# Request a weight load early, spread the Fourier chunks anew, and compute a tile plan with slots on partitions

## The chip, the cores and the metric

The kernel runs on one core of a Trainium2 chip. Its engines are TensorE (PE, matrix products), VectorE (DVE), ScalarE (ACT), GpSimd (POOL) and SyncE (SP, which issues most of the DMAs). Each engine has its own instruction queue and works through it in order; an instruction starts when the semaphores it waits for are set. The metric is device time in microseconds, the median of several runs.

## The reference

The input x is 8 x 3072 x 256. The reference takes the real part of a two-dimensional Fourier transform over each batch, 24,576 rows of 256 in all. Then come two layers. The first is a switched mixture of experts with a skip:

```python
do_compute = x @ w_skip > 0
e_idx = argmax(x[do_compute] @ w_gate)          # 8 experts, one is chosen
h = maximum(xc[mask] @ w1[e], 0)                # 256 -> 1024
y[mask] = gate_w * (h @ w2[e]);  out[do_compute] = xc + y
```

The second is applied to every row: h = x @ w_in (256 -> 2048), g = P(h) / Q(h) with a cubic P and Q = 1 + |b0||h| + |b1|h^2, and g @ w_out (2048 -> 256).

## The kernel before, in words

All products are made from f16 pairs (high and low part), three products for one.

**Fourier stage (lines 455 to 692).** A loop over n runs 12 steps for each of the 8 batches, plus two. In step gp of batch bb, `s2` transforms the features of a pair of column groups (product into u, ACT evicts o2h, DVE makes o2l), `s3` finishes the sequence direction two steps later, and its rows are written to a row buffer, one of ten places, of which seven lie in the memory mw that later holds expert weights. `s1` makes a chunk of the first stage for the next batch, eight chunks to a batch; `go` (line 635) says in which steps. ACT writes the chunk's high half (`s1_hi`, line 242) and, in the step after the chunk, the low half o1l (`s1_lo`, line 253). The tile u has three buffers, used by `s1` and `s2` in turn. `decode_steps` (line 391) converts w_in and w_out and the first two experts into f16 pairs in DRAM (WD), 65 small steps spread over 84 loop steps; each piece is loaded on SP into one of two buffers wr.

**Routing.** When a batch is done, `route_steps` (line 334) runs one segment per loop step beside the next batch: expert choice on DVE, a counting product on PE (line 354), the row numbers si, and then 24 scatters of rows to XS in DRAM by POOL (line 380), two in a step, three for the last batch. A `tick` (line 379) is a copy on POOL that reads an earlier step's o2h and so holds the scatters back. The last batch's segments run in the second part.

**Second part (from line 696).** The loop over i (line 1196) makes the second layer in steps of 256 of the 2048 columns: `z_mm1` (u), T, Y, V on ACT and DVE, gh and gl on DVE, a subtraction V on POOL, and `z_mm2` five steps later into accz, with the result ob evicted at the end of a tile. Between these it runs `all_moe`, the experts on halves of 256 rows: a DMA of rows xm, weights into mw (`load_moe`, line 880), a split and a DMA transpose (`moe_begin`), products e and acc. `last` is the routing of the last batch, `planning` the generator `make_plan` (line 727). The plan says for each of 52 slots which rows and which expert come next, and later the same for up to 116 left-over slots; it is computed on DVE, on one partition, with the slots along the free dimension (1x416 and 1x928 elements). Between both plans `fill` (line 902) copies rows on SP when all scatters are issued. The first three halves of expert 0 are loaded before the plan is known; the first load of weights, `WD[0]` (line 889), goes into the place of four of the row buffers.

The order on each engine is the order of these calls; no planner changes it.

Of the kernel before, what the change touches and what calls it, by code (L numbers as in the profile page):

```python
# [33 lines left out]
S1 = 52  # L34
# [18 lines left out]
def constants():  # L53
# [57 lines left out]
    c["lt8"] = (np.arange(8)[None, :] < np.arange(8)[:, None]).astype(np.float32).reshape(1, 64)  # L111
# [20 lines left out]
def program(tc, x, w_skip, w_gate, w1, w2, w_in, w_out, a, b, f1, cs, tw, tok, ut, small, lt8, slot, out):  # L132
# [3 lines left out]
    with es:  # L136
# [197 lines left out]
        def route_steps(bb, new_u, per=2):  # L334
# [16 lines left out]
            yield  # L351
            u = new_u()
# [18 lines left out]
            yield  # L371
# [3 lines left out]
            yield  # L375
            for g in range(NG):
                if g % per == 0 and bb < B - 1:

                    pool.tensor_copy(out=tick[:].bitcast(F16)[:, 0:1], in_=seen[0][:, 0, 0:1])
                i = pool.indirect_dma_start(out=XS[:, :], out_offset=IndirectOffsetOnAxis(ap=si[:, g:g + 1], axis=0),  # L380
                                            in_=rws[g // 4][:, g % 4, :], in_offset=None, bounds_check=NROWS - 1, oob_is_err=False)
                if scat:
                    tc.declare_no_dep(i.ins, group="scat", reason="every slot is given once")
                tc.add_to_no_dep_group("scat", i.ins)
                if bb >= 4:
                    tc.add_to_no_dep_group("scat7", i.ins)
                scat.append(i.ins)
                if g % per == per - 1:
                    yield

        def decode_steps():
# [10 lines left out]

            nxt = load(0)
# [29 lines left out]
            def load_e(n):  # L433
                e, k = divmod(n, 4)
                t = wp.tile([128, 2048], I32, tag="wr", bufs=2, name="wr")[:].bitcast(F32)[:, 0:1024]
                if k < 2:
                    sp.dma_start(out=t, in_=w1[e, k * 128:k * 128 + 128, :])
                else:
                    sp.dma_start(out=t.rearrange("p (c n) -> p c n", c=4), in_=w2[e, (k - 2) * 512:(k - 1) * 512, :].rearrange("(c p) n -> p c n", p=128))
                return t  # L440

            nxt = load_e(0)
# [268 lines left out]
        pll = pool_of("pll", 1)  # L711
# [14 lines left out]

        def make_plan():
            def v(n, name):
                return pl.tile([1, n], F32, name=name)

            pf = v(NC_, "pf")
            sl_t, lt_t = v(NL + S1, "sl_t"), v(64, "lt_t")
            lim, fs = sl_t[:, NL:NL + S1], v(1, "fs")
            sp.dma_start(out=sl_t[:], in_=slot)
            sp.dma_start(out=lt_t[:], in_=lt8)
            cnt, nt, pad, cx, px, ce, r2 = (v(n, nm) for n, nm in ((9, "cnt"), (8, "nt"), (8, "pad"), (8, "cx"), (8, "px"), (8, "ce"), (8, "r2")))
            ti = pl.tile([1, 8], I32, name="ti")
            m8, mt, pt, tk, tf, of, st, t1 = (v(n, nm) for n, nm in ((64, "m8"), (1, "mt"), (1, "pt"), (1, "tk"), (1, "tf"), (1, "of"), (1, "st"), (1, "t1")))
            ind = rt[0:1, 0:NL * 8]
            sA, sB, sC = v(NL, "sA"), v(NL, "sB"), v(NL, "sC")  # L740
            sm = pll.tile([1, NL], F32, name="sm")
# [3 lines left out]
            def floor_of(dst, src, add, shift):  # L745
                n = src.shape[-1]
                ts(out=ti[:, 0:n], in0=src, scalar1=float(add), scalar2=None, op0=ALU.add)
                ts(out=ti[:, 0:n], in0=ti[:, 0:n], scalar1=shift, scalar2=None, op0=ALU.logical_shift_right)
                dve.tensor_copy(out=dst, in_=ti[:, 0:n])

            def before(dst, src):
                m = m8[:].rearrange("o (e f) -> o e f", f=8)
                tt(out=m, in0=src[:, None, :].to_broadcast([1, 8, 8]), in1=lt_t[:].rearrange("o (e f) -> o e f", f=8), op=ALU.mult)
                dve.tensor_reduce(out=dst[:, :, None], in_=m, op=ALU.add, axis=AX.X)

            tt(out=cnt[:], in0=carry[0:1, :], in1=smt[0:1, 0:9], op=ALU.subtract)
            tt(out=cnt[:], in0=cnt[:], in1=smt[0:1, 9:18], op=ALU.mult)
# [16 lines left out]
            stt(out=r2[:], in0=cx[:], scalar=-float(HALF), in1=smt[0:1, 9:17], op0=ALU.mult, op1=ALU.mult)  # L774
            tt(out=r2[:], in0=r2[:], in1=smt[0:1, 26:34], op=ALU.add)

            def skip_row(dst, s, limit, unit, tmp):
                ts(out=tmp, in0=s, scalar1=limit, scalar2=None, op0=ALU.is_lt)
                ts(out=dst, in0=s, scalar1=float(unit), scalar2=nsk, op0=ALU.mult, op1=ALU.subtract)
                tt(out=dst, in0=dst, in1=tmp, op=ALU.mult)  # L780
                ts(out=dst, in0=dst, scalar1=nsk, scalar2=float(SKIP0), op0=ALU.add, op1=ALU.add)

            def halves(rows, experts, s, n, at):

                b3 = [1, n, 8]
                i3 = ind[:, 0:8 * n].rearrange("o (m e) -> o m e", e=8)
                v3 = rt[0:1, at:at + 8 * n].rearrange("o (m e) -> o m e", e=8)
                s3 = s[:, :, None].to_broadcast(b3)
                tt(out=i3, in0=s3, in1=cx[:, None, :].to_broadcast(b3), op=ALU.is_ge)
                tt(out=v3, in0=s3, in1=ce[:, None, :].to_broadcast(b3), op=ALU.is_ge)  # L790
                yield
                tt(out=i3, in0=i3, in1=v3, op=ALU.subtract)
                stt(out=v3, in0=s3, scalar=float(HALF), in1=smt[0:1, None, 9:17].to_broadcast(b3), op0=ALU.mult, op1=ALU.mult)
                tt(out=v3, in0=v3, in1=r2[:, None, :].to_broadcast(b3), op=ALU.add)
                yield
                tt(out=v3, in0=v3, in1=i3, op=ALU.mult)
                dve.tensor_reduce(out=sA[:, 0:n, None], in_=v3, op=ALU.add, axis=AX.X)
                yield
                tt(out=v3, in0=i3, in1=smt[0:1, None, 34:42].to_broadcast(b3), op=ALU.mult)
                dve.tensor_reduce(out=experts[:, :, None], in_=v3, op=ALU.add, axis=AX.X)  # L800
                yield
                ts(out=sC[:, 0:n], in0=s, scalar1=mt[:], scalar2=of[:], op0=ALU.subtract, op1=ALU.add)
                skip_row(rt[0:1, at:at + n], sC[:, 0:n], tk[:], HALF, sB[:, 0:n])
# [10 lines left out]
            stt(out=m8[:, 0:8], in0=pad[:], scalar=-float(HALF), in1=smt[0:1, 50:58], op0=ALU.add, op1=ALU.mult)  # L814
            tt(out=px[:], in0=px[:], in1=m8[:, 0:8], op=ALU.add)
            stt(out=px[:], in0=tk[:].to_broadcast([1, 8]), scalar=float(HALF), in1=px[:], op0=ALU.mult, op1=ALU.add)
            ts(out=pf[:, C_SRC:C_SRC + 8], in0=px[:], scalar1=nsk, scalar2=float(SKIP0), op0=ALU.min, op1=ALU.add)
            tt(out=pad[:], in0=cnt[:, 0:8], in1=smt[0:1, 9:17], op=ALU.mult)
            tt(out=pf[:, C_DST:C_DST + 8], in0=pad[:], in1=smt[0:1, 42:50], op=ALU.add)
            ts(out=pf[:, C_DUM:C_DUM + 1], in0=nsk, scalar1=float(SKIP0), scalar2=None, op0=ALU.add)  # L820
            out_now(C_SRC, C_DUM + 1)
            yield
            skip_row(pf[:, C_SKIP:C_SKIP + S2], sl_t[:, 0:S2], tf[:], TILE, sB[:, 0:S2])
            out_now(C_SKIP, C_SRC)
            yield from halves(pf[:, C_ROW:C_ROW + S1], pf[:, C_EXP:C_EXP + S1], sl_t[:, 0:S1], S1, 576)

            ex = pf[:, C_EXP:C_EXP + S1]
            tt(out=sA[:, 0:S1], in0=ex, in1=lim, op=ALU.is_le)
            dve.tensor_reduce(out=fs[:], in_=sA[:, 0:S1], op=ALU.min, axis=AX.X)
# [9 lines left out]
            tt(out=fs[:], in0=fs[:], in1=co[0:1, 16:17], op=ALU.mult)  # L839
            fast = fs[:]  # L840
            tt(out=of[:], in0=of[:], in1=fast, op=ALU.mult)
            ts(out=st[:], in0=fast, scalar1=float(S1), scalar2=None, op0=ALU.mult)
            ts(out=sm[:], in0=sl_t[:, 0:NL], scalar1=st[:], scalar2=None, op0=ALU.add)
            yield from halves(pf[:, C_LROW:C_LROW + NL], pf[:, C_LEXP:C_LEXP + NL], sm[:], NL, NL * 8)
# [4 lines left out]
            floor_of(pf[:, C_REM:C_REM + 1], t1[:], 1, 1)  # L849
# [30 lines left out]
        def load_moe(m):  # L880
# [418 lines left out]
```

## Time and profile before

| | us |
|---|---|
| median of 3 runs (3045.4 to 3047.98) | 3046.88 |
| profiled execution | 3047.06 |
| its span, first to last instruction | 3045.3 |
| PE busy (96% of the span) | 2911.8 |
| DVE busy (92%) | 2797.9 |
| ACT busy (84%) | 2549.3 |
| POOL busy (45%) | 1384.9 |

Busy shares are averages over stages with different limits: each stage is read from its own rows. The span and the profiled execution differ by what lies before the first and after the last instruction, 1.8 us.

### The profile page before, as it was taken

How to read it: one execution, taken by the hardware profiler on the slowest of the kernel's cores; microseconds unless marked ns; L12 is line 12 of the kernel's file. 1: busy time of each engine (PE TensorE's matmuls, PEld its weight loads, DVE VectorE, ACT ScalarE, POOL GpSimd, SP SyncE). 2: the span in 40 equal slices, each digit the busy share in tenths (PEclk: the TensorE clock that was granted, in tenths of full speed). 3: DMA queues.
4: the chain of work that ended last, by engine and by line, in shares of the span. 5: the costliest groups of instructions: out<-in, count | busy, mean ns of one | idle time of the engine just before them, and what ended most of it. 6: DMA issues, size and time to landing. Idle time of an engine off the chain costs nothing.

```text
span 3045.3 us, 57147 instructions
## 1 busy us (share of the span) xinstructions
PE 2911.8 (96%) x22994; PEld 2132.2 (70%) x22994; DVE 2797.9 (92%) x2909; ACT 2549.3 (84%) x2835; POOL 1384.9 (45%) x861
## 2 busy tenths in 40 slices
PE   7898868999899999999999999999999999999995
PEld 6777746776677777777777777777777777777764
DVE  6888769999999999999999999998999989999896
ACT  6887767888788988988889888888888888888884
POOL 0476665444344444444444444434444444444444
PEclk9999989999999999999999999999999999999998
DMA  7666653223121331323222121121122111210100
GB/s 207 192 183 187 240 150 88 77 63 111 43 70 46 94 91 42 71 72 102 56 56 84 53 46 36 50 76 33 38 63 71 28 44 27 91 39 25 36 15 15
DMA packets 230370, 236.87 MB, mean 78 GB/s; under 512 B 166995, under 2 KB 190932, under 8 KB 227156
## 3 DMA queue, kind: packets, MB, share of 16 engines
q1 hardware_dynamic: 209364, 174.23, 21.3%
q0 software_dynamic: 18432, 50.55, 4.7%
q10 hardware_dynamic: 2304, 8.39, 0.7%
q8 instruction: 181, 2.97, 0.4%
q14 instruction: 89, 0.73, 0.1%
HBM read 190.69 MB, written 77.05 MB: 88 GB/s over the span
## 4 chain that ended last, share of the span: by engine, by line
PE 75%; DVE 13%; ACT 4%; DMA 4%; issue 3%; POOL 1%; SPq 0%; ACTq 0%; POOLq 0%; DVEq 0%
PE accz L948 28%; PE u L938 27%; PE acc L948 8%; PE e L938 8%; DVE gh L1042 3%; PE u L269 2%; DVE T L1024 2%; DVE V L1047 2%; DMA out<-ob,ids 2%; DVE gl L1054 1%; PE v L319 1%; DVE wo L211 1%; DVE o2l L274 1%; ACT wo L204 1%; ACT o2h L273 0%
## 5 line engine op out<-in xcount | busy, mean ns | idle before, releaser
L1048 POOL TENSOR_TENSOR V<-T,V 128x1024 f32<-128x1024 f32 x384 | 913.7, 2379 | 1374.0 <-DVE V L1047 1373.6
L938 PE MATMUL u<-turned,wi 128*128 128x512 f16 x4608 | 1064.3, 381 | 20.6 <-DVE T L1024 17.8
L948 PE MATMUL accz<-wo,gh 128*128 128x256 f16 x6144 | 1034.9, 274 | 9.2 <-ACT ob L1070 9.2
L948 PE MATMUL accz<-wo,gl 128*128 128x256 f16 x3072 | 841.1, 274 | 20.0 <-DVE gl L1054 17.7
L1042 DVE SCALAR_TENSOR_TENSOR gh<-T,co,Y 128x1024 f16<-128x1024 f32 x384 | 803.2, 2092 | 0.0
L938 PEld LDWEIGHTS <-wi 128*128 128x128 f16 x4608 | 452.6, 98 | 490.0 <-issue 31.8
L1022 ACT ACTIVATE T<-u,co 128x1024 f32<-128x1024 f32 x384 | 462.9, 1205 | 328.8 <-PE u L938 210.5
L948 PEld LDWEIGHTS <-gh 128*128 128x128 f16 x6144 | 603.7, 98 | 162.6 <-issue 10.3
L1024 DVE SCALAR_TENSOR_TENSOR T<-T,co,u 128x1024 f32<-128x1024 f32 x384 | 487.6, 1270 | 66.0 <-ACT Y L1023 65.5
L1054 DVE SCALAR_TENSOR_TENSOR gl<-V,co,Y 128x1024 f16<-128x1024 f32 x384 | 489.1, 1274 | 28.8 <-POOL V L1048 28.8
L1047 DVE SCALAR_TENSOR_TENSOR V<-V,co,gh 128x1024 f32<-128x1024 f32 x384 | 490.3, 1277 | 0.0
L1028 ACT ACTIVATE V<-Y,co 128x1024 f32<-128x1024 f32 x384 | 440.4, 1147 | 23.7 <-DVE gl L1054 23.7
L1032 ACT ACTIVATE Y<-V,co 128x1024 f32<-128x1024 f32 x384 | 441.2, 1149 | 0.0
L1023 ACT ACTIVATE Y<-u,co 128x1024 f32<-128x1024 f32 x384 | 426.3, 1110 | 0.0
L1036 ACT ACTIVATE Y<-Y 128x1024 f32<-128x1024 f32 x384 | 404.3, 1053 | 0.0
L948 PEld LDWEIGHTS <-gl 128*128 128x128 f16 x3072 | 301.7, 98 | 59.9 <-DVE gl L1054 21.6
L938 PE MATMUL e<-turned,mw 128*128 128x256 f16 x2496 | 307.7, 273 | 15.0 <-DMA turned<-rows 15.0
L948 PE MATMUL acc<-mw,hh 128*128 128x256 f16 x1664 | 278.1, 273 | 0.0
L938 PEld LDWEIGHTS <-mw 128*128 128x128 f16 x2496 | 244.7, 98 | 44.2 <-DMA mw<-wd 12.2
L1071 POOL DMA_INDIRECT out<-ob,ids x192 | 232.8, 1213 | 64.2 <-issue 44.7
L948 PE MATMUL acc<-mw,hl 128*128 128x256 f16 x832 | 226.8, 273 | 0.0
L948 PEld LDWEIGHTS <-hh 128*128 128x128 f16 x1664 | 162.8, 98 | 18.9
(207 smaller groups left out, 2739.1 us busy)
## 6 DMA issues: line engine op xcount, KB each, us to landing
mw<-wd SPq DMA_DIRECT2D x50, 2048.0 KB
wi<-in_x SPq DMA_DIRECT2D x64, 384.0 KB
xm<-xs SPq DMA_DIRECT2D x52, 258.0 KB
wf<-in_moe_w SPq DMA_DIRECT2D x48, 256.0 KB
wd<-ws SPq DMA_DIRECT2D x48, 256.0 KB
xt<-xs SPq DMA_DIRECT2D x22, 516.0 KB
wd<-ws ACTq DMA_DIRECT2D x16, 512.0 KB
wr<-in_moe_w_in SPq DMA_DIRECT2D x4, 1024.0 KB
```

What stands on the lines that cost most here:

```text
L938: pe.matmul(u[:, s, :], lhsT=sta, rhs=mv[:, :, k, :], start=(n == 0), stop=(n == 5))
L948: pe.matmul(acc[:, r, :], lhsT=sta[:, c], rhs=mv, start=(first and r % 2 == 0 and s == 0 and n == 0), stop=(last and s == nf - 1 and n == ...
L1022: act.activation(d["T"], d["u"], AF.Square, scale=A[0], bias=A[1])
L1023: act.activation(d["Y"], d["u"], AF.Abs, scale=A[4])
L1024: dve.scalar_tensor_tensor(out=d["T"], in0=d["T"], scalar=A[2], in1=d["u"], op0=ALU.add, op1=ALU.mult)
L1028: act.activation(d["V"], d["Y"], AF.Square, bias=A[5])
L1032: act.activation(d["Y"], d["V"], AF.Ln, bias=A[6])
L1036: act.activation(d["Y"], d["Y"], AF.Exp, scale=-1.0)
L1042: dve.scalar_tensor_tensor(out=h[:], in0=d["T"], scalar=A[a0], in1=d["Y"], op0=ALU.add, op1=ALU.mult)
L1047: dve.scalar_tensor_tensor(out=d["V"], in0=d["V"], scalar=A[c], in1=h[:], op0=ALU.add, op1=ALU.mult)
L1048: pool.tensor_tensor(out=d["V"], in0=d["T"], in1=d["V"], op=ALU.subtract)
L1054: dve.scalar_tensor_tensor(out=l[:], in0=d["V"], scalar=A[a0], in1=d["Y"], op0=ALU.add, op1=ALU.mult)
```

## The change

Four edits. (1) The routing gets one more step between the one-hot and the counting product, except for batch 6 (`hurry`), which loses three steps, has no ticks and issues four scatters in a step. (2) The decoder's first load is issued in step 0, and the first load of the expert weights in its last decode piece. (3) Chunks are made in steps 0-2, 4-6, 8 and 9 of a batch instead of 0, 1, 3, 4, 6, 7, 9 and 10. (4) In the second part the constants sl_t and lt_t are loaded at the head, the first expert's weights in two DMAs, and the plan is computed with one slot to a partition; its two columns (row, expert) go to DRAM and come back as rows. One scalar takes the same way before the second plan. Constants for it: `small[:, 58]` is the partition's number, and lt8 is repeated on 128 partitions.

```diff
@@ route_steps
+            hurry = bb == B - 2
...
-            yield
+            if not hurry:
+                yield
...
             yield
+            if not hurry:
+                yield
             u = new_u()
...
+            if hurry:
+                per = 4
             for g in range(NG):
-                if g % per == 0 and bb < B - 1:
+                if g % per == 0 and bb < B - 2:
@@ decode_steps
             nxt = load(0)
-            pend = None
+            yield
             for n in range(8):
                 t = nxt
-                if n + 1 < 8:
-                    nxt = load(n + 1)
+                nxt = load(n + 1) if n + 1 < 8 else load_e(0)
...
-            nxt = load_e(0)
             for n in range(4 * EARLY):
@@ Fourier loop
-            go = c1 < 8 * B and gp % 3 != 2
+            go = c1 < 8 * B and gp % 4 != 3 and gp < 10
...
+            if n == 0:
+                next(prep)
@@ second part
+        sl_t = pl.tile([1, NL + S1], F32, name="sl_t")
+        lt_t = pl.tile([128, 64], F32, name="lt_t")
+        sp.dma_start(out=sl_t[:], in_=slot)
+        sp.dma_start(out=lt_t[:], in_=lt8)
+        PD = tc.dram_tile([128, 2], F32, name="pd")
+        PF = tc.dram_tile([1, 1], F32, name="pfs")
@@ make_plan (its tiles are now [128, n])
+            def halves(s, n, to):
+                sH, sC, hA, hB, ro = (hw[:, k:k + 1] for k in range(5))
+                ts(out=hi[:], in0=cx[:], scalar1=s, scalar2=None, op0=ALU.is_le)
+                stt(out=hi[:], in0=ce[:], scalar=s, in1=hi[:], op0=ALU.is_gt, op1=ALU.mult)
+                ts(out=sH, in0=s, scalar1=float(HALF), scalar2=None, op0=ALU.mult)
+                stt(out=hv[:, 0:8], in0=smt[:, 9:17], scalar=sH, in1=r2[:], op0=ALU.mult, op1=ALU.add)
+                yield
+                dve.tensor_copy(out=hv[:, 8:16], in_=smt[:, 34:42])
+                v3 = hv[:].rearrange("p (t e) -> p t e", e=8)
+                tt(out=v3, in0=v3, in1=hi[:, None, :].to_broadcast([128, 2, 8]), op=ALU.mult)
+                dve.tensor_reduce(out=hc[:, :, None], in_=v3, op=ALU.add, axis=AX.X)
+                ts(out=sC, in0=s, scalar1=mt[:], scalar2=of[:], op0=ALU.subtract, op1=ALU.add)
+                yield
+                skip_row(ro, sC, tk[:], HALF, hA)
+                stt(out=hB, in0=s, scalar=mt[:], in1=ro, op0=ALU.is_ge, op1=ALU.mult)
+                tt(out=hc[:, 0:1], in0=hc[:, 0:1], in1=hB, op=ALU.add)
+                sp.dma_start(out=PD[:, :], in_=hc[:])
+                sp.dma_start(out=to.rearrange("o (c n) -> o c n", c=2), in_=PD[0:n, None, :].rearrange("n o c -> o c n"))
...
+            yield from halves(smt[:, 58:59], S1, pf[0:1, C_ROW:C_ROW + 2 * S1])
+            for _ in range(3):
+                yield
...
+            sp.dma_start(out=PF[:, :], in_=fs[0:1])
+            sp.dma_start(out=fs[:], in_=PF[0:1, 0:1].to_broadcast([128, 1]))
+            for _ in range(3):
+                yield
...
+            yield from halves(st[:], NL, pf[0:1, C_LROW:C_LROW + 2 * NL])
+            for _ in range(3):
+                yield
@@ load_moe
-                    sp.dma_start(out=w, in_=WD[0])
+                    for k in (0, 2):
+                        sp.dma_start(out=w[:, k:k + 2], in_=WD[0, :, k:k + 2])
```

## Rows read from the trace of the kernel before

**Rows 1.** Windows by stage: bounds, length, busy us (instructions) by engine, clock, DMA.
```profile
0.00:394.80 394.80, 343.10 (x4153) 284.97 (x4154) 302.59 (x717) 303.94 (x506) 194.86 (x236) 0.97 0.65 198
394.80:511.40 116.60, 81.79 (x506) 50.74 (x505) 90.76 (x153) 73.16 (x78) 65.70 (x59) 0.87 0.39 119
...
730.00:810.00 80.00, 67.39 (x489) 47.29 (x487) 79.35 (x83) 58.01 (x60) 29.11 (x16) 1.00 0.24 74
810.00:2950.00 2140.00, 2138.30 (x15834) 1548.97 (x15832) 2046.16 (x1733) 1869.74 (x1940) 953.97 (x481) 1.00 0.20 56
```

**Rows 2.** Windows of steps 5 to 8 of batches 0, 1, 2, 5.
```profile
49.49:70.90 21.41, 16.56 (x178) 13.15 (x176) 11.52 (x19) 14.12 (x23) 0.00 (x0) 0.84 0.77 246
102.47:115.93 13.46, 12.95 (x158) 10.70 (x156) 12.97 (x41) 11.80 (x20) 4.52 (x6) 1.00 0.51 146
146.33:162.15 15.82, 13.32 (x158) 10.90 (x158) 14.21 (x42) 12.87 (x22) 9.39 (x12) 1.00 0.54 163
...
282.03:304.01 21.98, 15.28 (x177) 12.20 (x175) 12.72 (x42) 13.92 (x22) 8.56 (x13) 0.84 0.63 196
```

**Rows 3.** Waits, 30 to 345 us: who for whom, total us, times, longest.
```profile
DVE wf L415 <- DMA wr<-in_moe_w_in: 6.5, 1, 6.5
...
ACT ws L448 <- DMA wr<-in_moe_w: 5.7, 1, 5.7
```

**Rows 4.** Timeline of PE: start, length, instruction, idle time before and its releaser.
```profile
212.53 0.40 PE L269 MATMUL u<-f2t,o1h 128*128 128x276 f16 x2 [0.60 <-ACT o1l L253]
...
216.95 0.29 PE L269 MATMUL u<-f2t,o1l 128*128 128x276 f16 x1 [1.23 <-ACT o1l L253]
...
431.56 2.72 PE L938 MATMUL e<-turned,mw 128*128 128x256 f16 x12 [15.01 <-DMA turned<-rows]
```

**Rows 5.** Waits of PE, 30 to 396 us.
```profile
PE u L269 <- ACT o1l L253: 11.6, 13, 1.2
```

**Rows 6.** Waits of PE, 395 to 520 us.
```profile
PE u L938 <- DVE T L1024: 9.3, 5, 3.0
PE accz L948 <- ACT ob L1070: 5.2, 1, 5.2
...
PE acc L354 <- DVE rt L350: 2.4, 1, 2.4
```

**Rows 7.** Timeline of POOL, scatters from 371 to 416 us.
```profile
371.40 1.13 POOL L380 DMA_INDIRECT xs<-mw,rt  x1 [6.87 <-DMA xt<-xs]
...
415.84 0.97 POOL L380 DMA_INDIRECT xs<-mw,rt  x1 [0.30 <-issue]
```

**Rows 8.** Timeline of SP's issues, 418 to 505 us.
```profile
418.74 0.33 SPq L889 DMA_DIRECT2D mw<-wd  x1
...
421.83 4.44 SPq L929 DMA_TRANSPOSE turned<-rows  x1
...
426.85 0.23 SPq L735 DMA_DIRECT2D lt_t<-const_lt  x1
...
489.64 0.64 SPq L906 DMA_DIRECT2D xs<-dum  x1
...
503.98 0.38 SPq L885 DMA_DIRECT2D xm<-xs  x1
```

**Rows 9.** Timeline of DVE at the first plan.
```profile
431.76 0.21 DVE L753 TENSOR_TENSOR m<-nt,lt_t 1x64 f32<-1x64 f32 x1 [7.46 <-DMA lt_t<-const_lt]
```

**Rows 10.** DVE by line, 731 to 783 us: busy us, mean ns, idle before.
```profile
L1042 DVE SCALAR_TENSOR_TENSOR gh<-T,co,Y 128x1024 f16<-128x1024 f32 x5 | 6.3, 1267 | 0.0
...
L790 DVE TENSOR_TENSOR rt<-sm,ce 1x928 f32<-1x928 f32 x1 | 3.3, 3278 | 0.0
...
L789 DVE TENSOR_TENSOR rt<-sm,cx 1x928 f32<-1x928 f32 x1 | 1.1, 1111 | 0.0
...
L846 DVE TENSOR_TENSOR t<-t,of 1x1 f32<-1x1 f32 x1 | 0.1, 148 | 0.0
```

**Rows 11.** DVE by line, 520 to 1000 us.
```profile
L1042 DVE SCALAR_TENSOR_TENSOR gh<-T,co,Y 128x1024 f16<-128x1024 f32 x70 | 147.2, 2103 | 0.0
```

More of the change, by code (lines that the diff above doesn't have):

```diff
@@ L110, in constants @@
     c["small"] = np.broadcast_to(small, (128, 64)).copy()
-    c["lt8"] = (np.arange(8)[None, :] < np.arange(8)[:, None]).astype(np.float32).reshape(1, 64)
+    c["small"][:, 58] = np.arange(128)
+    c["lt8"] = np.broadcast_to((np.arange(8)[None, :] < np.arange(8)[:, None]).astype(np.float32).reshape(1, 64), (128, 64)).copy()
     c["slot"] = np.concatenate([np.arange(NL), [limit(m) for m in range(S1)]]).astype(np.float32).reshape(1, NL + S1)
@@ L370, in route_steps @@
                 dve.tensor_scalar(out=carry[:, 0:1], in0=carry[:, 0:1], scalar1=float(R1 * HALF), scalar2=None, op0=ALU.max)
-            yield
+            if not hurry:
+                yield
             dve.tensor_tensor(out=rk, in0=rk, in1=oh, op=ALU.mult)
@@ L401, in load, with load_e @@
                 return t
+            def load_e(n):
+                e, k = divmod(n, 4)
+                t = wp.tile([128, 2048], I32, tag="wr", bufs=2, name="wr")[:].bitcast(F32)[:, 0:1024]
+                if k < 2:
+                    sp.dma_start(out=t, in_=w1[e, k * 128:k * 128 + 128, :])
+                else:
+                    sp.dma_start(out=t.rearrange("p (c n) -> p c n", c=4), in_=w2[e, (k - 2) * 512:(k - 1) * 512, :].rearrange("(c p) n -> p c n", p=128))
+                return t
             nxt = load(0)
-            pend = None
+            yield
             for n in range(8):
                 t = nxt
-                if n + 1 < 8:
-                    nxt = load(n + 1)
+                nxt = load(n + 1) if n + 1 < 8 else load_e(0)
                 v = t[:].rearrange("p (n two) -> p n two", two=2)
@@ L710, in program @@
         pl = pool_of("pl", 1)
-        pll = pool_of("pll", 1)
         obp = pool_of("obp", 1)
@@ L725, in program @@
         plan = pl.tile([1, NC_], I32, name="plan")
+        sl_t = pl.tile([1, NL + S1], F32, name="sl_t")
[4 more added lines that the diff above has]
+        PF = tc.dram_tile([1, 1], F32, name="pfs")
         def make_plan():
             def v(n, name):
-                return pl.tile([1, n], F32, name=name)
-            pf = v(NC_, "pf")
-            sl_t, lt_t = v(NL + S1, "sl_t"), v(64, "lt_t")
+                return pl.tile([128, n], F32, name=name)
+            pf = pl.tile([1, NC_], F32, name="pf")
+            hi, hv, hc, hw = v(8, "hi"), v(16, "hv"), v(2, "hc"), v(5, "hw")
             lim, fs = sl_t[:, NL:NL + S1], v(1, "fs")
-            sp.dma_start(out=sl_t[:], in_=slot)
-            sp.dma_start(out=lt_t[:], in_=lt8)
             cnt, nt, pad, cx, px, ce, r2 = (v(n, nm) for n, nm in ((9, "cnt"), (8, "nt"), (8, "pad"), (8, "cx"), (8, "px"), (8, "ce"), (8, "r2")))
-            ti = pl.tile([1, 8], I32, name="ti")
+            ti = pl.tile([128, 8], I32, name="ti")
             m8, mt, pt, tk, tf, of, st, t1 = (v(n, nm) for n, nm in ((64, "m8"), (1, "mt"), (1, "pt"), (1, "tk"), (1, "tf"), (1, "of"), (1, "st"), (1, "t1")))
-            ind = rt[0:1, 0:NL * 8]
-            sA, sB, sC = v(NL, "sA"), v(NL, "sB"), v(NL, "sC")
-            sm = pll.tile([1, NL], F32, name="sm")
+            sA, sB = v(S1, "sA"), v(S1, "sB")
             nsk = cnt[:, 8:9]
@@ L746, in floor_of @@
                 n = src.shape[-1]
-                ts(out=ti[:, 0:n], in0=src, scalar1=float(add), scalar2=None, op0=ALU.add)
-                ts(out=ti[:, 0:n], in0=ti[:, 0:n], scalar1=shift, scalar2=None, op0=ALU.logical_shift_right)
-                dve.tensor_copy(out=dst, in_=ti[:, 0:n])
+                t = ti[0:src.shape[0], 0:n]
+                ts(out=t, in0=src, scalar1=float(add), scalar2=None, op0=ALU.add)
+                ts(out=t, in0=t, scalar1=shift, scalar2=None, op0=ALU.logical_shift_right)
+                dve.tensor_copy(out=dst, in_=t)
             def before(dst, src):
                 m = m8[:].rearrange("o (e f) -> o e f", f=8)
-                tt(out=m, in0=src[:, None, :].to_broadcast([1, 8, 8]), in1=lt_t[:].rearrange("o (e f) -> o e f", f=8), op=ALU.mult)
+                tt(out=m, in0=src[:, None, :].to_broadcast([128, 8, 8]), in1=lt_t[:].rearrange("o (e f) -> o e f", f=8), op=ALU.mult)
                 dve.tensor_reduce(out=dst[:, :, None], in_=m, op=ALU.add, axis=AX.X)
-            tt(out=cnt[:], in0=carry[0:1, :], in1=smt[0:1, 0:9], op=ALU.subtract)
-            tt(out=cnt[:], in0=cnt[:], in1=smt[0:1, 9:18], op=ALU.mult)
+            tt(out=cnt[:], in0=carry[:], in1=smt[:, 0:9], op=ALU.subtract)
+            tt(out=cnt[:], in0=cnt[:], in1=smt[:, 9:18], op=ALU.mult)
             floor_of(nt[:], cnt[:, 0:8], HALF - 1, 8)
@@ L773, in make_plan @@
             yield
[L774 to L775 removed]
+            stt(out=r2[:], in0=cx[:], scalar=-float(HALF), in1=smt[:, 9:17], op0=ALU.mult, op1=ALU.mult)
+            tt(out=r2[:], in0=r2[:], in1=smt[:, 26:34], op=ALU.add)
             def skip_row(dst, s, limit, unit, tmp):
+                n = nsk[0:s.shape[0]]
                 ts(out=tmp, in0=s, scalar1=limit, scalar2=None, op0=ALU.is_lt)
[L779 removed]
+                ts(out=dst, in0=s, scalar1=float(unit), scalar2=n, op0=ALU.mult, op1=ALU.subtract)
@@ L813, in make_plan @@
             yield
[L814 to L820, printed above, removed]
+            one = nsk[0:1]
+            stt(out=m8[0:1, 0:8], in0=pad[0:1], scalar=-float(HALF), in1=smt[0:1, 50:58], op0=ALU.add, op1=ALU.mult)
+            tt(out=px[0:1], in0=px[0:1], in1=m8[0:1, 0:8], op=ALU.add)
+            stt(out=px[0:1], in0=tk[0:1].to_broadcast([1, 8]), scalar=float(HALF), in1=px[0:1], op0=ALU.mult, op1=ALU.add)
+            ts(out=pf[:, C_SRC:C_SRC + 8], in0=px[0:1], scalar1=one, scalar2=float(SKIP0), op0=ALU.min, op1=ALU.add)
+            tt(out=pad[0:1], in0=cnt[0:1, 0:8], in1=smt[0:1, 9:17], op=ALU.mult)
+            tt(out=pf[:, C_DST:C_DST + 8], in0=pad[0:1], in1=smt[0:1, 42:50], op=ALU.add)
+            ts(out=pf[:, C_DUM:C_DUM + 1], in0=one, scalar1=float(SKIP0), scalar2=None, op0=ALU.add)
             out_now(C_SRC, C_DUM + 1)
             yield
-            skip_row(pf[:, C_SKIP:C_SKIP + S2], sl_t[:, 0:S2], tf[:], TILE, sB[:, 0:S2])
+            skip_row(pf[:, C_SKIP:C_SKIP + S2], sl_t[:, 0:S2], tf[0:1], TILE, sB[0:1, 0:S2])
             out_now(C_SKIP, C_SRC)
-            yield from halves(pf[:, C_ROW:C_ROW + S1], pf[:, C_EXP:C_EXP + S1], sl_t[:, 0:S1], S1, 576)
+            yield from halves(smt[:, 58:59], S1, pf[0:1, C_ROW:C_ROW + 2 * S1])
+            for _ in range(3):
+                yield
             ex = pf[:, C_EXP:C_EXP + S1]
-            tt(out=sA[:, 0:S1], in0=ex, in1=lim, op=ALU.is_le)
-            dve.tensor_reduce(out=fs[:], in_=sA[:, 0:S1], op=ALU.min, axis=AX.X)
+            tt(out=sA[0:1], in0=ex, in1=lim, op=ALU.is_le)
+            dve.tensor_reduce(out=fs[0:1], in_=sA[0:1], op=ALU.min, axis=AX.X)
             tt(out=ex, in0=ex, in1=lim, op=ALU.min)
@@ L837, in make_plan @@
                 yield
-            tt(out=fs[:], in0=fs[:], in1=co[0:1, 16:17], op=ALU.mult)
+            sp.dma_start(out=PF[:, :], in_=fs[0:1])
+            sp.dma_start(out=fs[:], in_=PF[0:1, 0:1].to_broadcast([128, 1]))
+            for _ in range(3):
+                yield
+            tt(out=fs[:], in0=fs[:], in1=co[:, 16:17], op=ALU.mult)
             fast = fs[:]
             tt(out=of[:], in0=of[:], in1=fast, op=ALU.mult)
-            ts(out=st[:], in0=fast, scalar1=float(S1), scalar2=None, op0=ALU.mult)
-            ts(out=sm[:], in0=sl_t[:, 0:NL], scalar1=st[:], scalar2=None, op0=ALU.add)
-            yield from halves(pf[:, C_LROW:C_LROW + NL], pf[:, C_LEXP:C_LEXP + NL], sm[:], NL, NL * 8)
+            stt(out=st[:], in0=fast, scalar=float(S1), in1=smt[:, 58:59], op0=ALU.mult, op1=ALU.add)
+            yield
+            yield from halves(st[:], NL, pf[0:1, C_LROW:C_LROW + 2 * NL])
+            for _ in range(3):
+                yield
             tt(out=t1[:], in0=mt[:], in1=tk[:], op=ALU.add)
```

34 lines of the change are left out of this document (2 added, 32 removed).

## The prediction

> **What bounds the kernel now.** I read the windows by stage first. From 810 to 2950 us TensorE is busy 2138.3 of 2140, so time can only be won where PE stands idle or runs at its lower clock. Three stretches do that [rows 1]: the Fourier stage (PE 343.1 busy of 394.8 us), the opening of the second part (81.79 of 116.6, mean granted clock 0.87) and the second plan (67.39 of 80). The change edits these three. In each I then read who ends PE's waits. The profiled execution took 3047.06 us (span 3045.3), the median of the runs is 3046.88; the sum starts from 3047.
>
> **Weight loads in the Fourier stage.** Two loads are requested in the step that uses them: the first of w_in, for which DVE stands 6.5 us, and the first of w1, for which ACT stands 5.7 us [rows 3]. Both engines are in order, so o2h and o2l behind them, and then PE, stand too. Steps 5 to 8 of those two batches took 21.41 and 21.98 us; the same steps of the four batches between took 13.46 to 15.82, mean 14.84 [rows 2]. The excess is 6.6 + 7.1 = 13.7 us, and the granted clock is 0.84 there against 1.00. After the change the first load leaves SP in step 0, five steps earlier, the other six decode yields earlier, and neither takes a buffer that is still being read. On SP it passes a few x loads, which are requested four chunks ahead. I take the waits themselves, 6.5 + 5.7 = **12.2 us gained**; bounds 8 (a third of it late elsewhere) and 13.7.
>
> **Chunks in steps 0-2, 4-6, 8, 9.** Now the last chunk of a batch is in step 10; ACT writes its low half at the end of step 11 and the next batch's first product needs it: PE stands 1.23 us [rows 4], at seven batch boundaries some 8.5 us of the 11.6 that it waits for o1l in all [rows 5]. With the last chunk in step 9 a step is to spare. Against it: u has three buffers, and after two chunk steps in a row PE's next product waits for ACT's o1l of the step before; one such wait was 0.60 us [rows 4]. Today four steps of a batch follow such a pair (2, 5, 8, 11), then five do (2, 3, 6, 7, 10): 7 x 0.6 = 4.2 us back. I take **5 us gained**; bounds 8.5 gained, and 4 lost (three more such waits per batch, 12.6, against 8.5).
>
> **The routing of a batch.** The extra yield puts the counting of batches 0 to 5 and their 24 scatters one step later on PE, DVE and POOL; the rows that they free are rewritten later still. For the last but one batch three yields go, and the ticks (small POOL copies that hold scatters back). But POOL has no pause there: from 371.40 to the issue at 415.84 it makes 34 scatters, 1.3 us each [rows 7], tick or no tick, so the last of them leave it when they do now. For steps 84 to 97 I take **0**; bounds 4 either way, since the later scatters of batch 5 meet the 4 MB of weights loaded there, and POOL already stood 6.87 us for the DMA queue at 371.40.
>
> **The opening.** PE's waits are 15.0 us for the first expert's turned rows [rows 4], 9.3 for DVE's T, 5.2 for ob and 2.4 for the routing's one-hot [rows 6].
> The first: SP issues the expert's 2 MB at 418.74, after the last scatter that reads their place, the transpose at 421.83, and PE starts at 431.56 [rows 4, 8], 9.7 us later, behind those 2 MB. In two parts, the one with w1 waits only for the scatters up to group 15, eight scatters or 10 us earlier, and 1 MB is left in front of the transpose: 5 us off.
> The second and fourth: scatters that free the last batch's rows come 2 to 3 us sooner in POOL's order, which takes the 2.4. DVE stands 7.46 us for lt_t [rows 9], which SP requests at 426.85, behind the transpose [rows 8]; at the head of the second part it is there in time. DVE's chain then starts ten us earlier, and its first plan loses nine operations over 416 elements (416/928 of 1.11 us [rows 10], 0.5 each). Of the 9.3 I leave 4.5, since DVE stays the later engine until the plan is done.
> The third: xm is issued at 503.98 behind the fill, which holds SP from 489.64 after the last scatter [rows 8]. One yield more puts that scatter into iteration 9, where xm is issued ahead of the fill; of 5.2 I leave 1.5.
> The clock: 0.87 over 116.6 us is some 30 us at 1.2 instead of 2.4 GHz; with half of the idle time gone I take 3 us back. Sum 5 + 2.4 + 4.8 + 3.7 + 3 = 18.9, less 1 for the detour below: **18 us gained**; bounds 8 and 25.
>
> The plan now turns columns into rows through DRAM: a write and a read on SP, the read waiting for the write, and DVE's next plan step for the read. Behind them on SP stand the next iteration's transposes and row loads. The nearest row is lt_t, 0.2 KB on a full queue: 4.9 us from 426.85 to DVE's start at 431.76 [rows 8, 9], two of them 9.8. In the first plan T, gh, gl, V and hl stand between, some 5.5 us at 1.27 each [rows 10], so DVE waits 0 to 4.4; I take 1. In the second plan three whole iterations cover it. The Trainium skill speaks against detours in small pieces ("DMA: Bandwidth & Descriptors", section "Anatomy of one DMA"): about 2 us of a DMA do not depend on its size. By that the round trip is an estimated 4 us, DVE would not wait and the sum would be 1 us better; the full queue's row is worse than the page.
>
> **The second plan.** PE loses 80 - 67.39 = 12.6 us [rows 1] with DVE 79.35 busy. The plan's operations take DVE 23.5 us: three like L790 (2.95 to 3.28 us), two of 2.0, six like L789 (1.11) and eighteen small ones like L846 (0.15 to 0.27) [rows 10]. Slots now lie on partitions, so each operation is over 8 elements or 1: some 26 like L846, 4.4 us. But the 23.5 are not all plan. L789 and L790 have the same size and took 1.11 and 3.28 us; and gh took 1.27 in this stretch [rows 10], 2.10 elsewhere [rows 11]. A stall strikes once an iteration whoever meets POOL's V; with the plan small it falls on gh again, 6 x 0.83 = 5 us. So the plan costs 18.5 net, and 18.5 - 4.4 = 14.1 go. By shares that is 12.6 x 14.1/18.5 = 9.6 of PE's idle time; if the remaining 4.4 fit beside PE, all 12.6. I take **10.5 us gained**; bounds 4 and 12.6.
> The Trainium skill's "SBUF — State Buffer", section "Who interferes with whom", gives the reason: a DVE operation with two SBUF inputs shares a port pair with GpSimd, and the second to come waits for the whole of the first. By that rule the stall stays as I have it; by busy times alone 19.1 us would go and the sum would be 2 us better. The rows above agree with the rule.
>
> **Sum.** 12.2 + 5 + 0 + 18 + 10.5 = 45.7; 3047 - 46 = **3001 us**.
>
> **Rivals.**
> - *ACT sets the pace of the chunks.* Three chunk steps in a row keep ACT behind PE: chunks lose 4, steps 84 to 97 lose 4: 3047 - 12.2 + 4 + 4 - 18 - 10.5 = 3014. For it: ACT is 304 of 394.8 busy [rows 1]. Against it: the total is the same, and steps 10 and 11 have no chunk.
> - *The first expert stays late.* POOL has the same 34 scatters, so the second half of the weights and the transpose go out as now, and the 9.7 us after it are the queue's, not the load's. Then the opening gains 8: 3011.
> - *The detour costs.* Round trips as slow as two of lt_t's: 5 us more, 3006.
> - *Slower: SP's head is blocked.* sl_t and lt_t are now the first DMAs of the second part. If their place is memory that the last batch's rows still occupy, they wait for the last scatter, landed by 489.64, and first rows, weights and transpose wait behind them. From weights to the first product SP needs 12.8 us (418.74 to 431.56), so the expert starts at 503, +71, less the 14.5 us of later waits that vanish in it and the 27.7 gained elsewhere: 3076. It decides from a start of these loads at about 460 on. Against it: the same pool gave them before, and lt_t went out at 426.85 with no such wait.
>
> **How the numbers follow.** Forecast 0.55, ACT's pace 0.17, late expert 0.17, detour 0.05, blocked SP 0.06. The forecast's own range is 2988 to 3014. For 8 in 10 it is stretched to both middle rivals together on the one side (45.7 - 13 - 10 = 23 gained, 3024, and some) and to the upper bounds of opening and chunks with part of the rest on the other: 2984 to 3027. About 0.2% (6 us) can be told from no change: faster by more 0.91, within 0.03, slower 0.06, the blocked queue.
>
> **What would show it.** Right: no wait for wr on DVE and ACT; no 1.2 us wait at batch boundaries; the first e product some 5 us earlier after the stage's end; no wait for lt_t; the fill behind xm; PE full during the second plan, whose operations stay under 0.3 us where V doesn't stall them. Wrong: new waits of PE for o1l in steps 3 and 7 of over 8 us; DVE standing for the plan's read; SP standing at sl_t. The forecast falls if the opening is not at least 8 us shorter.

## The result

The changed kernel takes 3022.15 us (median, 3017.47 to 3023.02), the kernel before 3047.24 in the same group of runs: ratio 0.9917, interval 0.9905 to 0.9928, or 25 us gained. I had forecast 46, with a range of 2984 to 3027 us. The profiled execution took 3023.02 us, its span is 3021.2.

Three points on PE's timeline locate the gain: the end of the last `s3` product (end of the Fourier stage), the start of the 15th group of second-layer products (opening over, plan 1 done) and the start of the 101st (plan 2 done).

```
us from the span's start    stage end   15th group   101st group
kernel before                 394.85       517.00       1106.22
changed kernel                395.97       499.07       1082.44
length, before / after     394.85/395.97  122.15/103.10  589.22/583.37
```

The Fourier stage gained nothing (1.1 us lost, 17.2 gained in the forecast), the opening 19.0 (18 forecast), the second plan 5.9 (10.5 forecast). The windows of the changed kernel that answer to [rows 1], columns as there (its second window reaches to the 15th group; the one of before ends 5.6 us ahead of it):

```profile
0.00:396.00 396.00, 342.42 (x4153) 287.25 (x4154) 303.30 (x720) 303.96 (x507) 205.53 (x240) 0.97 0.67 201
396.00:499.10 103.10, 81.18 (x542) 52.99 (x542) 89.74 (x149) 75.95 (x80) 61.46 (x44) 0.92 0.38 117
712.60:786.10 73.50, 68.81 (x499) 48.83 (x497) 73.12 (x75) 59.46 (x62) 30.85 (x18) 0.98 0.29 87
786.10:2926.10 2140.00, 2137.95 (x15822) 1548.24 (x15821) 2044.20 (x1738) 1867.75 (x1937) 951.29 (x481) 1.00 0.20 56
```

PE is busy for 342 to 343 us of the stage in both kernels, so what the earlier weight loads freed was spent on something else. No wait for wr is left on DVE, and 0.4 us on ACT, where [rows 3] had 6.5 and 5.7. But ACT, which writes the rows of a step into their buffer, now stands for scatters that still read that buffer. ACT's waits, 34 to 394 us (total, times, longest), first in the kernel before:

```profile
ACT mw L322 <- DMA xs<-mw,rt: 4.3, 4, 2.3
```

and in the changed kernel, 26.7 us in sum:

```profile
ACT third L323 <- DMA xs<-third,rt: 15.4, 4, 6.0
ACT mw L323 <- DMA xs<-mw,rt: 11.3, 5, 4.4
```

Three of these on ACT's timeline of the changed kernel; the number in brackets is the idle time before the instruction:

```profile
346.53 0.39 ACT L323 ACTIVATE mw<-v 128x258 f32<-128x258 f32 x1 [4.37 <-DMA xs<-mw,rt]
...
380.87 0.39 ACT L323 ACTIVATE third<-v 128x258 f32<-128x258 f32 x1 [3.33 <-DMA xs<-third,rt]
...
388.76 0.39 ACT L323 ACTIVATE third<-v 128x258 f32<-128x258 f32 x1 [6.05 <-DMA xs<-third,rt]
```

With the rows of step 8 of batches 2 to 6 ACT began to rewrite one half of a row buffer 7.6 to 16.3 us after POOL's last scatter of that half in the kernel before, and 5.1 to 7.3 us after it in the changed one (read off the timelines of POOL and ACT). Batch 4 in the kernel before:

```profile
248.90 1.26 POOL L380 DMA_INDIRECT xs<-mw,rt  x1 [0.30 <-ACT o1l L253]
...
256.59 0.38 ACT L322 ACTIVATE mw<-v 128x258 f32<-128x258 f32 x1
```

and in the changed kernel:

```profile
242.79 0.98 POOL L388 DMA_INDIRECT xs<-mw,rt  x1 [0.30 <-ACT o1h L243]
...
247.85 0.39 ACT L323 ACTIVATE mw<-v 128x258 f32<-128x258 f32 x1
```

The yield that I priced at nothing moved the 24 scatters of each of batches 0 to 5 one step later, into the time that ACT had to spare.

### The profile page after: what moved, and what is told of

Its sections match the earlier page's. It is cut to its first block, busy times and chain, and to the rows that moved or that the text cites. A ratio compares the mean times of both kernels' runs of the same rounds, so it can differ in the third digit from the quotient of the medians.

```text
span 3021.2 us, 57147 instructions
## 1 busy us (share of the span) xinstructions
PE 2907.7 (96%) x22994; PEld 2134.0 (71%) x22994; DVE 2786.6 (92%) x2902; ACT 2548.8 (84%) x2835; POOL 1387.1 (46%) x849
## 4 chain that ended last, share of the span: by engine, by line
PE 73%; DVE 15%; issue 4%; DMA 4%; ACT 2%; POOL 1%; SPq 0%; POOLq 0%; ACTq 0%; DVEq 0%
PE u L954 27%; PE accz L964 27%; PE acc L964 8%; PE e L954 8%; DVE gh L1058 4%; DVE T L1040 2%; DVE V L1063 2%; DMA out<-ob,ids 2%; PE u L270 1%; DVE gl L1070 1%; DMA xs<-mw,rt 1%; DVE wo L212 1%; POOL xs L388 1%; DVE hl L972 1%; DMA xs<-third,rt 1%
## 5 line engine op out<-in xcount | busy, mean ns | idle before, releaser
L954 PE MATMUL u<-turned,wi 128*128 128x512 f16 x4608 | 1059.4, 380 | 12.7 <-DVE T L1040 10.5
```

The costliest lines, as they stand in the source:

```text
L954: pe.matmul(u[:, s, :], lhsT=sta, rhs=mv[:, :, k, :], start=(n == 0), stop=(n == 5))
```

## The experiments

The first four ran on a chip on which the kernel before took 3048.6 us. The other eight ran in two groups on other chips, where it took 3081.7 and 3080.8; so times are compared within a group, and ratios are to the kernel before in the same group.

**e1: the extra yield taken out.**

```diff
             yield
-            if not hurry:
+            if bb == B - 1:
                 yield
             u = new_u()
```

> The changed kernel without the yield that was added in the routing (batches 0 to 6; the last batch keeps it, since the opening rests on it). So the counting and the 24 scatters of batches 0 to 5 are one step earlier again. Theory: that yield eats the time between a scatter's issue and the rewriting of its row buffer, and ACT stands for scatters (26.7 us between 34 and 394 us in the changed kernel, 4.3 in the kernel before): ACT's wait for scatters falls under 10 us, the Fourier stage ends 8 to 14 us earlier, the opening keeps its gain, time 3008 to 3014 (changed kernel 3022). Rival A, the new places of the chunks cost it: time 3019 to 3025, ACT's waits stay over 20 us. Rival B, the hurried batch and the earlier weights of steps 84 to 97 cost it all: the stage before step 84 doesn't move, the time stays within 3 us.

3007.18 us (3005.37 to 3008.24), ratio 0.9866, interval 0.985 to 0.9881. The stage ends at 380.87, 15.1 us earlier; the opening is 101.7 us long, so that gain stays. ACT's waits for scatters in e1, 10.9 us in sum:

```profile
ACT mw L323 <- DMA xs<-mw,rt: 6.4, 4, 3.9
...
ACT third L323 <- DMA xs<-third,rt: 4.5, 3, 2.5
```

All three numbers lie just outside what I expected (3008 to 3014, 8 to 14 us, under 10 us). The one line costs 15 us; both rivals would have left it in place. By ACT's o2h of steps 60 and 84, 2.6 us of it came before step 60, 4.7 in steps 60 to 83 and 7.8 in steps 84 to 97, where POOL sends two batches' scatters in a row. By the start of PE's product of step 84 only 3.2 of the 15.1 had come, so most of the price falls due at the end.

**e2: the chunks in the old steps**, the yield kept (`gp % 3 != 2`).

> The changed kernel with the first-stage chunks in the old steps (all but 2, 5, 8, 11 of a batch). Theory (the yield is what costs): the 1.2 us waits at batch boundaries come back, some 5 us lost or, since the scatters' waits hide part of it, 0 to 5: 3022 to 3027. Rival A, the new places let ACT fall behind in batches 1 to 4 and 6: 4 to 10 us faster, 3012 to 3018, with ACT's waits for scatters under 15 us.

3023.52 us (ratio 0.9916, interval 0.9902 to 0.993): 1.4 us from the changed kernel. The stage ends at 398.07, 2.1 us later. ACT's waits for scatters are 20.5 us (34 to 394 us), not under 15 as rival A has it: the new places don't make ACT late. With the yield in they are worth some 2 us in the stage, not 5; in the time the two kernels can't be told apart.

**e3: the kernel before with the weight loads alone.**

```diff
             nxt = load(0)
+            yield
...
-                if n + 1 < 8:
-                    nxt = load(n + 1)
+                nxt = load(n + 1) if n + 1 < 8 else load_e(0)
...
+            if n == 0:
+                next(prep)
```

> The kernel before with the one edit that requests the weights ahead (first load in step 0, the first of w1 one load earlier). By the prediction's term 12.2 us: 3035. Theory: that holds, nothing else of the stage moves, 3033 to 3037. Rival: the earlier loads cost elsewhere or the gain is given back in steps 84 to 97, where POOL and the DMA queue set the pace: 3040 to 3047.

3030.81 us, ratio 0.9943, interval 0.9929 to 0.9956, faster than expected. The stage ends at 382.69, 12.16 us earlier: the term of 12.2. The opening is 3.0 us shorter as well (119.1), which I hadn't counted and can't explain. ACT's waits for scatters are 9.7 us here (34 to 394 us), against 4.3 in the kernel before: part of the rise in the changed kernel comes with the earlier loads alone.

**e4: the kernel before with the plan on partitions and its two tables alone.**

> The kernel before with the plan on partitions alone (with its two tables requested at the head of the second part); Fourier stage, routing and the first expert's weights as before. The prediction gave lt_t and the smaller first plan 4.8 us, less 1 for the detour, and the second plan 10.5; the two traces show 6.4 for the second. Theory: 10 to 14 gained, 3033 to 3037, of which 6 to 7 in the second plan. Rival: the detour holds DVE in the first plan and the opening gains nothing, 3040; or the plan of the changed kernel gave back 3.8 us only because of where its iterations fell, then the second plan gains 10 here, 3030.

3030.69 us, ratio 0.9944, interval 0.9931 to 0.9958. The opening is 8.0 us shorter (114.2), the second plan 7.5, the stage 0.8 longer. The time is the one that the last rival named, but not by its way: the second plan did not gain 10. So the two edits alone gained 17.8 and 17.9 us, 35.7 together if they add up, against 25 for the whole change: the rest of the change cost more than it gained.

**f1 to f4: parts of the rest, all without the extra yield.** f1 takes out every `hurry`; f2 has the old chunk steps; f3 loads WD[0] in one DMA; f4 takes the extra yield from the last batch too.

f1:

```diff
-            if not hurry:
-                yield
+            yield
...
-            if hurry:
-                per = 4
...
-                if g % per == 0 and bb < B - 2:
+                if g % per == 0 and bb < B - 1:
```

f2 and f3:

```diff
-            go = c1 < 8 * B and gp % 4 != 3 and gp < 10
+            go = c1 < 8 * B and gp % 3 != 2
```

```diff
-                    for k in (0, 2):
-                        sp.dma_start(out=w[:, k:k + 2], in_=WD[0, :, k:k + 2])
+                    sp.dma_start(out=w, in_=WD[0])
```

f4:

```diff
-            if bb == B - 1:
-                yield
```

> The changed kernel without the extra yield (median 3007.2, stage end at 380.9, 14.0 us ahead of the kernel before), and without the hurry of the last but one batch: its three yields, its ticks and two scatters per step are back. In its trace with the hurry PE stands 5.4 us for that batch's one-hot, 2.1 with the weights alone changed. Theory: the hurry costs the Fourier stage 3 to 4 us there, since PE's product is queued right behind DVE's one-hot, and pays in the opening, where rows of that batch gate the first expert: stage end 377 to 378, opening 3 to 6 us longer, time 3006 to 3011. Rival: the hurry gains nothing in the opening, since POOL's 34 scatters set their end: 3003 to 3005.

> The changed kernel without the extra yield, with the first-stage chunks in the old steps: the chunk term by itself, free of the yield. My prediction gave it 5 us. Theory: it is about 2 (what it showed with the yield, 3.2 against 1.1 at the stage's end), 3008 to 3011. Rival A: with the yield gone the full 5 to 8.5 us show, 3012 to 3016. Rival B: the new places gain nothing, 3005 to 3008.

> The changed kernel without the extra yield, with the first expert's weights in one load of 2 MB again. Theory: as in the prediction, the two parts are worth some 5 us of the wait for turned rows, since the one load waits for the last scatter that reads its place: the first expert's product 4 to 6 us later, 3010 to 3013. Rival: the transpose is held by the queue and not by the load, 3006 to 3009.

> The changed kernel without the extra yield in the last batch too. Theory: that yield puts the last scatter's step behind the request of xm, so that xm passes the fill; without it xm is issued behind the fill again and PE stands some 3 us more for ob (1.9 now, 5.2 in the kernel before): 3009 to 3012. Rival: the scatters of the last batch being a step earlier, the fill is earlier too and nothing is lost: 3005 to 3008.

None of the times could be held against e1, since the chip was another one. Their ratios are in the table below. Among themselves f3, which has all but the halves of the load, is 9.2 us faster than f2 and 6.8 faster than f4, and 14.9 slower than f1. The measure ran again, as g1, on a third chip, beside f1 (g2), f2 (g3) and g4, which gives the hurried batch its yields back and keeps its scatters:

```diff
-            if not hurry:
-                yield
+            yield
```

> The changed kernel without the extra yield once more, as the measure for the three beside it: the four runs of the last group fell on a chip on which the kernel before took 3081.7 us, so their times can't be set against the 3007.2 of the earlier run. Theory: ratio to the kernel before 0.985 to 0.988 on a chip like the first. On a chip like the last one it would be over 0.99, since steps 84 to 97 took 67 to 69 us there with the hurry.

> As f1, beside its measure. Theory: where TensorE isn't short of instructions the hurry costs 3 to 4 us before the stage's end and pays 6 to 11 in the opening (f1's opening, from the stage's end to the 15th group of products, was 112.9 us, the three hurried ones 100.3 to 105.1): 3 to 8 us slower than the measure. Rival: the hurried scatters cost steps 84 to 97 on every chip, then it is 10 us or more faster than the measure, as among the last four.

> As f2, beside its measure: the chunk term without the yield. f2 reached its stage's end 5 to 8 us later than f3 and f4, which have the same stage but for the chunks. Theory: 4 to 8 us slower than the measure. Rival: with a chip like the first 0 to 2, as between the changed kernel and e2.

> The measure with two of the three dropped yields of the last but one batch back; its scatters still go four to a step without ticks. Theory: the 5.4 us that TensorE stands for that batch's one-hot come from the merged steps; they fall to about 2, the scatters start a step later, which the opening feels as 1 to 3 us: within 3 us of the measure. Rival: the wait stays, since DVE is behind ACT there anyway, and the later scatters cost 3 to 6.

```
                                   us       ratio, interval          stage end  15th group  opening
g1 without the extra yield         3055.37  0.9914 (0.9899-0.9929)     432.08     532.08     100.0
g2 ... and without the hurry       3039.55  0.9866 (0.9851-0.9881)     404.96     517.75     112.8
g3 ... with the old chunk steps    3065.17  0.9947 (0.9933-0.996)      444.68     544.66     100.0
g4 ... hurried scatters only       3051.77  0.9905 (0.989-0.992)       426.60     526.61     100.0
f1                                 3041.76  0.9875 (0.986-0.9889)      404.76     517.64     112.9
f2                                 3065.82  0.9955 (0.9943-0.9966)     439.12     539.43     100.3
f3                                 3056.64  0.9918 (0.9906-0.9931)     430.90     531.78     100.9
f4                                 3063.40  0.9941 (0.9929-0.9954)     433.75     538.88     105.1
```

The chips of f and g can be compared by these points: f1 and g2 are one kernel, and f2 and g3 are one, and their openings differ by 0.1 and 0.3 us.

*Hurry.* (Against the kernel before, batch 6 loses two yields and is not given the third; I counted three lost ones.) On these chips it lengthens the stage by 27.1 us (g1 against g2), and the kernel is 15.8 us slower for it, as the rival had it (10 us or more), though on these chips alone. The opening is 12.8 us shorter, but it is counted from a stage end that came 27.1 us later. POOL itself is hardly ahead; its last scatter of batch 6 in g1:

```profile
418.61 0.98 POOL L388 DMA_INDIRECT xs<-mw,rt  x1 [0.30 <-issue]
```

and in g2:

```profile
420.77 0.98 POOL L383 DMA_INDIRECT xs<-mw,rt  x1 [0.30 <-issue]
```

g4 has g2's yields and differs from it only in the scatters (four to a step, no ticks); its stage is 21.6 us longer. So most of the price is the scatters' pace. The other 5.5 us are between g4 and g1, where the steps are merged; PE's wait for that batch's one-hot is 2.1 in g4 and 5.5 in g1, as I expected. That wait on e1's timeline of PE:

```profile
356.26 1.01 PE L359 MATMUL v<-rt,utt 128*128 128x216 f16 x5 [5.42 <-DVE rt L353]
```

and on e3's, without the hurry:

```profile
361.24 0.99 PE L354 MATMUL v<-rt,utt 128*128 128x216 f16 x5 [2.08 <-DVE rt L350]
```

*Chunks.* The old steps cost 9.8 us beside their measure (12.6 at the stage's end, 11.0 of them by step 60), above the 4 to 8 that I expected; PE's wait for o1l from 34 to 270 us is 9.6 there and 4.4 in g1.

*The first expert's weights.* f3 waits as long as g1 for its turned rows: PE's waits from 404 to 545 us in f3,

```profile
PE e L953 <- DMA turned<-rows: 8.1, 1, 8.1
```

and in g1:

```profile
PE e L954 <- DMA turned<-rows: 8.1, 1, 8.1
...
PE accz L964 <- ACT ob L1086: 1.9, 1, 1.9
```

The openings are 100.9 and 100.0 us long. But this pair can't show the term of 5 us, which was to come from one half waiting for fewer scatters: on these chips POOL's last scatter of batch 6 starts some 13.5 us before the stage's end, and the load goes out 1 us behind the first rows without any wait. f3's issue on SP:

```profile
433.89 0.33 SPq L904 DMA_DIRECT2D mw<-wd  x1
```

On the first chip the load does wait for scatters. SP's two issues in e1, merged in one row:

```profile
392.32 8.83 SPq L905 DMA_DIRECT2D mw<-wd  x2
```

There the first e product starts 15.0 to 15.7 us after that last scatter with one load (the kernel before, e3, e4), and 14.5 and 12.1 after it with two (the changed kernel, e1). So the halves may be worth 1 to 4 us there; no run has them alone. The view of f4 that answers to the two above has the price of the last batch's yield:

```profile
PE accz L962 <- ACT ob L1084: 5.2, 1, 5.2
```

3.3 us more than in g1 and 3.2 more than in f3, on f4's own chip (2.0), where I had forecast 3.7. f4's opening is some 4 us longer than f3's.

*What was not run.* g2 is the fastest of its group, and its ratio is that of e1 on the first chip (0.9866 both). Whether leaving out the hurry also pays on the first chip wasn't tried: there e1's steps 84 to 97 took 40.4 us (from ACT's o2h) against 67.6 in f3, so the hurry has far less to lose. e3, on the first chip and without the hurry, took 37.0: as far as these two can be compared, the hurry costs some 3 us of the stage there.

## Why the prediction was right in direction and half off in size

That 3022 lies in the wide range is luck: it is outside the forecast's own range (2988 to 3014), and the stretch to 3027 was made for two rivals, neither of which came.

**The step that failed** is "The routing of a batch". It said of the 24 scatters that are one step later "the rows that they free are rewritten later still", and took 0 for steps 84 to 97, with bounds of 4 us. From ACT's o2h of step 84 to the stage's end the kernel before took 36.3 us, the changed one 48.2 and e1 40.4. Without the yield the whole stage ends 15.1 us earlier (e1). The trace of before had the number: 7.6 us from the last scatter to the rewriting at the tightest place of batches 2 to 6, and 4.0 in batch 7. A step is some 3.7 us long (45 us to a batch of 12), so one yield leaves some 4 of the 7.6. That is no more than a scatter needs from issue to landing, by the median in the DMA view of the kernel before:

```profile
xs<-mw,rt POOLq DMA_INDIRECT x132, 3.9
...
xs<-third,rt POOLq DMA_INDIRECT x60, 3.6
```

ACT already waited 4.3 us in four places. The sentence was an argument from the order of the code, without a row. (The 6.87 us that it reads as a wait for the DMA queue are by [rows 7] a wait for one load, xt<-xs.) Put 15 in its place and the sum is 45.7 - 15.1 = 30.6, or 3016; what is still missing lies in the second plan (4.6) and the chunks (2.9), less 1.0 in the opening.

**Weight loads**: 12.2 forecast, 12.16 in the stage (e3). Here the waits were rows, on engines that PE follows.

**Chunks**: 5 forecast, 2.1 in the stage with the yield (e2), 9.8 without it on a slower chip (g3). The sign was right. PE's wait for o1l (30 to 396 us) is 8.4 us in the changed kernel and 23.9 in e2, so its end hardly shows in the stage; that waits for scatters hide the rest is argued, not shown, since no run has the chunks without the yield on the first chip.

**Opening**: 18 forecast, 19.0 measured, from other parts than I named. The plan and its tables brought 8.0 alone (3.8 forecast after the detour), xm 3.3 (3.7). What the hurry and the halves of the weights bring on the first chip no run shows by itself. PE's waits of the changed kernel, 395 to 500 us, that answer to [rows 4, 6]:

```profile
PE u L954 <- DVE T L1040: 8.7, 5, 3.0
PE e L954 <- DMA turned<-rows: 8.1, 1, 8.1
...
PE accz L964 <- ACT ob L1086: 2.0, 1, 2.0
```

The expert's rows went from 15.0 to 8.1, more than the 5 that I took off, and ob from 5.2 to 2.0. T went only from 9.3 to 8.7, where I had left 4.5. But this split is that of a stage which ends late. With the yield out (e1, 380 to 520 us) it is near the forecast of T, and the rows gain little:

```profile
PE e L954 <- DMA turned<-rows: 13.0, 1, 13.0
PE u L954 <- DVE T L1040: 4.2, 4, 1.7
```

The two waits together are 16.8 us in the changed kernel and 17.2 in e1, 24.3 before; the forecast had 14.5. So it is partly luck that the sum came out near. SP's issues that answer to [rows 8]:

```profile
394.64 0.41 SPq L736 DMA_DIRECT2D sl_t<-const_slot  x1
395.15 0.34 SPq L737 DMA_DIRECT2D lt_t<-const_lt  x1
...
481.66 0.35 SPq L900 DMA_DIRECT2D xm<-xs  x1
...
483.82 0.65 SPq L922 DMA_DIRECT2D xs<-dum  x1
```

sl_t is issued at once, which refutes the blocked SP; xm goes ahead of the fill, as forecast. The detour through DRAM costs one wait of DVE, where I had taken 1 us:

```profile
DVE sA L837 <- DMA pf<-pd: 1.4, 1, 1.4
```

From the issue of the write on SP,

```profile
454.03 0.33 SPq L813 DMA_DIRECT2D pd<-hc  x1
457.13 0.77 SPq L814 DMA_DIRECT2D pf<-pd  x1
```

to DVE's next plan operation at 460.77 the round trip took 6.7 us, between the 4 and the 9.8 that the prediction worked out. The granted clock of the opening rose from 0.87 to 0.92. From the stage's end to the 15th group PE was busy for 87.3 us before and 81.2 after, for the same products: 6.2 us, where I took 3.

**Second plan**: 10.5 forecast, 5.9 measured (7.5 in e4). The mechanism held in part: the stall that strikes whoever meets POOL's V does not go with the plan. But it did not fall on gh, as I had it; it fell on the small operations themselves. DVE by line, 700 to 792 us of the changed kernel, that answers to [rows 10]:

```profile
L793 DVE TENSOR_TENSOR hw<-hw 128x1 f32<-128x1 f32 x1 | 2.2, 2237 | 0.0
L862 DVE TENSOR_TENSOR t<-t,st 128x1 f32<-128x1 f32 x1 | 2.2, 2205 | 0.0
...
L799 DVE TENSOR_SCALAR hi<-cx,st 128x8 f32<-128x8 f32 x1 | 2.0, 2009 | 0.0
L804 DVE COPY hv<-smt 128x8 f32<-128x8 f32 x1 | 2.0, 2008 | 0.0
L852 DVE TENSOR_TENSOR fs<-fs,co 128x1 f32<-128x1 f32 x1 | 2.0, 1998 | 0.0
...
L861 DVE TENSOR_TENSOR t<-t,of 128x1 f32<-128x1 f32 x1 | 0.2, 159 | 0.0
```

Five operations over 1 or 8 elements to a partition took 2.0 to 2.2 us each; another of the same form took 0.16. Each of the five ends 0.01 to 0.03 us after the subtraction V that POOL ran beside it. One of them, POOL's V first:

```profile
751.89 2.35 POOL L1064 TENSOR_TENSOR V<-T,V 128x1024 f32<-128x1024 f32 x1 [6.14 <-DVE V L1063]
...
752.26 2.01 DVE L804 COPY hv<-smt 128x8 f32<-128x8 f32 x1
```

I had charged gh 6 x 0.83 = 5 us for the stall; the plan paid 5 x 1.9 = 9.5, and the 4.5 between them are about what the second plan fell short by (4.6). The Trainium skill's "SBUF — State Buffer", section "Who interferes with whom", names operations with two SBUF inputs for this, which was the rule that I used. It also names copy and tensor_scalar, in a mode in which they take both ports. L804 is a plain copy and L799 a tensor_scalar, and both stood as long as the others (2.0 us); whether they ran in that mode no row shows.

**Rivals.** ACT's pace of the chunks fell with e2 and g3; the blocked SP fell with sl_t's issue at 394.64, and the late expert, which left the opening 8 us of gain, with its 19; the detour cost 1.4 us. A rival for the yield was missing altogether.

## What to carry to other kernels

A step that moves is priced at both ends: when its inputs are there, and when the memory that it still reads is wanted again. Read the second as a number, from the last reader's issue to the next writer's start, and compare it with the length of a step before calling a delay free. And when one edit frees time in a stage, look for the wait with the least slack there, since it is what the next edit will hit.

## What was not expected of the hardware

On the two slower chips PE stood while POOL sent scatters back to back, and the profile names nothing that it waited for. One window in g1, with 24 of them and one tick:

```profile
390.00:424.00 34.00, 10.62 (x44) 3.88 (x42) 1.93 (x5) 2.65 (x6) 22.73 (x25) 0.58 0.26 94
```

Scatters of the same stretch on the first chip, in e1 (15 and two ticks):

```profile
362.00:380.90 18.90, 17.13 (x198) 14.81 (x196) 13.00 (x31) 12.06 (x26) 14.57 (x17) 1.00 0.37 114
```

and two to a step with ticks between them, on the slower chip, in g2 (14 and six ticks):

```profile
385.00:405.00 20.00, 15.90 (x150) 12.94 (x148) 10.53 (x25) 8.74 (x19) 13.22 (x20) 0.81 0.43 112
```

PE is busy for 10.6 of 34 us in g1, at a granted clock of 0.58; DVE and ACT are busy for 1.9 and 2.7. Most of PE's idle time is put down to "issue", that is, to nothing that the profile shows (PE's waits in g1, 364 to 432 us):

```profile
PE u L270 <- issue: 17.4, 18, 2.4
PE v L320 <- issue: 6.2, 10, 1.7
```

In steps 84 to 97 such waits come to 23.6 us in g1, 8.9 in g4 and 3.0 in g2, and in none of e1's. That the stage grows with the scatters' pace is shown by g4 against g2; what PE lacked, and why only these chips do it, stays open.
